# Levels 1 and 2 of the scores computed elementwise, from eight tokens side by side in a partition

## The chip, the cores and the metric

The kernel runs on one core of a Trainium2 chip. Times are device microseconds of that core. Before the change the median of three runs is 647.9 us (647.87 to 648.56). The engines are PE (matmuls), DVE (vector), ACT (scalar), POOL (GpSimd) and SP, which in this kernel computes nothing: it issues nearly all the DMAs, one after another, from one queue.

## The reference

```python
# r, k, v, w: 4 x 8 x 768 x 48 (batch, heads, tokens, head width); u: 8 x 48
for t in range(S):
    cur = np.einsum('bhd,bhe->bhde', u[None] * kt, vt)
    y[:, :, t] = np.einsum('bhd,bhde->bhe', rt, state + cur)
    state = wt[:, :, :, None] * state + np.einsum('bhd,bhe->bhde', kt, vt)
...
x = y.transpose(0, 2, 1, 3).reshape(B * S, H * D)   # 3072 x 384
h = x @ w_in                                        # 384 x 2048
out = (h * sigmoid(h)) @ w_out                      # 2048 x 384
```

A recurrence over the tokens of each head, in which the state decays by `w`, and then a two-layer network with a Silu on every token.

## The kernel before

The work is cut into 12 units: 128 tokens of two of the four batches, all 8 heads. For a unit the recurrence becomes a masked matrix of scores, tokens by tokens, for each head. Entry (query, key) is the sum over the head width of r times k times the product of all `w` between the two tokens. It is built by levels. Level l pairs the second half of every block of 2 << l tokens with its first half; before it is computed, queries in second halves and keys in first halves are multiplied by products of `w` that reach the middle of their block. Level 0 with the diagonal (the "bonus", which has `u`) is elementwise: a partition holds two neighbouring tokens, POOL multiplies (`bonus`, lines 398 to 410), DVE sums over the head width (`bonus_sum`, 412 to 419), four small DMAs move the sums to the partition of their key (422 to 425), ACT and DVE put them in order (`bonus_spread`, 440 to 445), and a predicated copy writes them into `score` (`bonus_write`, 447). Levels 1 to 6 are matmuls: `score_products` (519) runs 8 for a level, and two levels run together as a `burst` (601): 1 with 2, 3 with 4, 5 with 6. `keep_level` (609) copies a level from PSUM into `score` with a mask, on DVE. `grow_queries` (470, DVE) and `grow_keys` (476, POOL, with a copy on ACT in `odd_keys`, 458) multiply on to the next level, and `prepare` (587) makes the second level of a burst ready ahead of the first; `product` (383, POOL) makes the products of `w`. With `score` complete, `y` (655) multiplies scores and values, `update` (671) brings the state on, and `move_x` (707) takes the result to the network's layout with ten DMAs.

The network of a unit is `up` (752), eight steps of 12 matmul records each with a Silu on ACT into `gt`, and `quarter` (806), seven steps of 16 records that make the second product with fewer block products than the plain way, from sums that `sums` (796) forms on DVE.

The order is written by hand. For units 3 to 11 `mix` (725) lists groups of the recurrence's steps, and the loop at line 920 puts after each group as many network steps as `ROOM` (919) says: first the seven `quarter` steps of unit i - 2, then the eight `up` steps of unit i - 1. `sums` comes with the last four `up` steps, two of them with the last. Each engine works through its own instructions in this order. `y` comes in the last group, after all network steps. The loads of unit i + 2 (`load_blocks`, 97, 48 DMAs) are spread over the groups (line 742), and `load_rk` (128) brings r and k of the next unit for the bonus. All these, `move_x`, the bonus moves and the stores of the output are on SP's queue in the order of the program. Units 0 to 2 have an order of their own (861 to 917).

Of the kernel before, what the change touches and what calls it, by code (L numbers as in the profile page):

```python
# [8 lines left out]
F32 = mybir.dt.float32  # L9
BF16 = mybir.dt.bfloat16  # L10
I8 = mybir.dt.int8
I32 = mybir.dt.int32
# [26 lines left out]
def kernel(  # L39
# [11 lines left out]
    nc = tc.nc  # L51
# [14 lines left out]
    units = [(n, b0) for n in range(S // L) for b0 in range(0, B, NB)]  # L66
    NSLOT = 2
    NTOK = 2


    const = ctx.enter_context(tc.tile_pool(name="const", bufs=1))
# [15 lines left out]
    def load_twos(to, src, i, queues):  # L87
        n, b0 = units[i]
        for b in range(NB):
            queues[b].dma_start(out=to[b * L // 2:(b + 1) * L // 2],  # L90
                                in_=src[b0 + b, :, n * L:(n + 1) * L, :].rearrange("h (i s) d -> i h (s d)", s=2))
# [35 lines left out]

    def load_rk(i):

        for x, src in enumerate((r, k)):  # L130
            load_twos(tokens_rk[:, x].rearrange("p h s d -> p h (s d)"), src, i, [nc.sync] * NB)


    rounding = ExitStack()
# [19 lines left out]
    own = const.tile([128, NOWN, 2 * PW], U32, name="own")  # L154

    tokens_rk = const.tile([128, 2, H, 2, D], F32, name="tokens_rk")

    def rk(i, x):
        if i < NTOK:
# [77 lines left out]
    warm = const.tile([128, 1], F32, name="warm")  # L237
    nc.scalar.activation(out=warm, in_=zero, func=AF.Silu)
    u_bc = const.tile([128, H, D], F32, name="u_bc")
    nc.sync.dma_start(out=u_bc, in_=u.partition_broadcast(128))  # L240
    load_weight(0)
    load_tokens(1)
# [140 lines left out]
    def product(i, l, engine=nc.gpsimd):  # L383
        t = tw[i][l]
        up = pt.tile([128, Q, L >> (l + 1)], F32, name=f"tw{l + 1}", bufs=2 if l == NL - 1 else 1)
        engine.tensor_tensor(out=up, in0=t[:, :, 0::2], in1=t[:, :, 1::2], op=ALU.mult)  # L386
        tw[i].append(up)
# [24 lines left out]
    def bonus_sum(i, x):  # L412
# [10 lines left out]
        for b in range(NB):  # L423
            for s in range(2):
                nc.sync.dma_start(out=diag[i][b][s::2], in_=own_sums[b * L // 2:(b + 1) * L // 2, s])

    def bonus_spread(i):

        if i < NTOK:
            if i == 0:  # L430
                diag[i] = p_w[:, 0, 0:NB * H * 2].rearrange("p (b h s) -> p b h s", b=NB, h=H)
            else:
                diag[i] = ps.tile([128, NB, H, 2], F32, name="p_m", bufs=2)
            for b in range(NB):
                for s in range(2):
                    nc.tensor.matmul(diag[i][:, b].rearrange("p h s -> p (h s)"), lhsT=spread[:, s, b, :],
                                     rhs=own_sums[:, s].rearrange("p h s -> p (h s)"), start=(b == 0 and s == 0),
                                     stop=(b == NB - 1 and s == 1))
            return
        both_b = pt.tile([128, NB, H, 2], F32, name="both_b", bufs=1)  # L440
        nc.scalar.copy(out=both_b[:, 0], in_=diag[i][0])
        for g in range(4):
            nc.scalar.copy(out=both_b[(3 - g) * 32:(4 - g) * 32, 1], in_=diag[i][1][g * 32:(g + 1) * 32])
        nc.vector.stream_shuffle(out=both_b[:, 1], in_=both_b[:, 1], mask=list(range(31, -1, -1)))
        diag[i] = both_b
# [8 lines left out]
    def keys(i, start, *dims):  # L454
        k = tk[i][:]
        return bass.AP(tensor=k.tensor, offset=k.offset + start, ap=[k.ap[0], *dims])
# [16 lines left out]
        nc.vector.tensor_tensor(out=odd, in0=odd, in1=tw[i][l][:, :, 0::2][:, :, :, None].to_broadcast([128, Q, L >> (l + 1), c]),  # L473
                                op=ALU.mult)

    def grow_keys(i, l):
        c, ni = 1 << l, L >> (l + 1)
        x_at, next_at = X[l % 2], X[(l + 1) % 2]
        for b in range(NB):
            row0 = NP + b * NP  # L480
            if l + 1 < NL:
                start = [next_at * L, row0 * L][b] + b * c
                step = 2 * c + (1 - 2 * b) * (row0 - next_at) * L
                out = keys(i, start, [4 * c, NP * ni // 2], [step, 2], [1, c])
                have = keys(i, x_at * L + b * c, [4 * c, NP * ni // 2], [2 * c, 2], [1, c])
                blocks = [[4, NP * ni // 2], [2, 2]]
            else:
                out = keys(i, row0 * L + b * c, [L, NP], [1, c])
                have = keys(i, x_at * L + b * c, [L, NP], [1, c])
                blocks = [[2, NP]]  # L490
            nc.gpsimd.tensor_tensor(out=out, in0=have, in1=odd_products(i, l, b, *blocks), op=ALU.mult)  # L491
        if i < NTOK:
            product(i, l)

    def odd_ones(i):

# [200 lines left out]
    def dense_x(i, b):  # L697

        if b == 0:
            xt[i] = pt.tile([128, KC, TU], F32, name="xt")  # L700
        p_x = ps.tile([128, KC, L], F32, name="p_h" if i == 0 else "p_m", bufs=2)
        for x, (c, p) in enumerate(parts):
            nc.tensor.matmul(p_x[:, c, :], lhsT=dense[:, x, :], rhs=yt[i][:, p, b, :],  # L703
                             start=(x == 0), stop=(x == len(parts) - 1))
        (nc.vector.tensor_copy if (i, b) == (0, 1) else nc.scalar.copy)(out=xt[i][:, :, b * L:(b + 1) * L], in_=p_x)

    def move_x(i):

        xt[i] = pt.tile([128, KC, TU], F32, name="xt")
        for h in range(H):  # L710
            at = h * D
            while at < (h + 1) * D:
                end = min((h + 1) * D, (at // 128 + 1) * 128)
                row = PD * (h % 2) + at - h * D
                nc.sync.dma_start(out=xt[i][at % 128:at % 128 + end - at, at // 128, :],
                                  in_=yt[i][row:row + end - at, h // 2].rearrange("p b t -> p (b t)"))
                at = end

    def both(fn, i, *args):
        return [(fn, i, b, *args) for b in range(NB)]  # L720
# [4 lines left out]
    def mix(i):  # L725

        groups = [[*both(turn, i, "w"), (product, i, 0)],
                  [*both(turn, i, "k"), *both(turn, i, "r"), (odd_ones, i)], [(start_levels, i), (prepare_keys, i, 1)],
                  [(prepare, i, 1), *[(product, i, l) for l in range(1, NL)]],
                  [(burst, i, 1), (keep_level, i, 1)], [(keep_level, i, 2), (go_on, i, 2)],  # L730
                  [(prepare, i, 3), (reverse_v, i), (bonus, i, 0)],
                  [(burst, i, 3), (keep_level, i, 3), (bonus_sum, i, 0), (bonus, i, 1), (bonus, i, 2)],
                  [(keep_level, i, 4), (go_on, i, 4)],
                  [(prepare, i, 5), (bonus_sum, i, 1)] + ([(load_rk, i + 1)] if i + 1 < len(units) else []),
                  [(burst, i, 5), (keep_level, i, 5)], [(keep_level, i, 6), (go_on, i, 6), (bonus_spread, i), (bonus_write, i)],
                  both(turn_k, i), [*both(y_state, i), *both(y, i), *both(update, i), (move_x, i)]]

        loads = block_loads(i + NSLOT) if i + NSLOT < len(units) else []
        if i + 1 < len(units):
            loads.insert(len(loads) // 2, (load_values, i + 1))  # L740

        behind = groups[3 if i > NTOK + 1 else 10:]
        for at, group in enumerate(behind):
            group += loads[at * len(loads) // len(behind):(at + 1) * len(loads) // len(behind)]
        return groups
# [6 lines left out]
    def up(i, m):  # L752
        p_h = ps.tile([128, 2, TU], F32, name="p_h", bufs=2)
        for a in range(2):
            f = 2 * m + a
            for c in range(KC):
                nc.tensor.matmul(p_h[:, a, :], lhsT=w_in_sb[:, c, f * 128:(f + 1) * 128], rhs=xt[i][:, c, :],  # L757
                                 start=(c == 0), stop=(c == KC - 1))
        if i == 0 and m < NFIRST:
            gt[i, m] = own[:, NOWN - 1, m * 2 * TU:(m + 1) * 2 * TU].bitcast(F32).rearrange("p (a t) -> p a t", a=2)  # L760
        else:
            gt[i, m] = pt.tile([128, 2, TU], F32, name="gt", bufs=FC // 2 + 3)
        nc.scalar.activation(out=gt[i, m], in_=p_h, func=AF.Silu)  # L763

    def out_room(b):
# [138 lines left out]
    for m in range(6):  # L904
# [7 lines left out]
    do(blocks[2], (burst, 2, 3), (keep_level, 2, 3), (keep_level, 2, 4), (go_on, 2, 4), (prepare, 2, 5), (bonus, 2, 1),  # L912
       (bonus, 2, 2), (down, 0, 1, 2), (bonus_sum, 2, 1), (load_rk, 3), (sums, 1, 1), *blocks[3:7], (down, 0, 1, 3))
    do((burst, 2, 5), (keep_level, 2, 5), (keep_level, 2, 6), (go_on, 2, 6), (up, 1, 6), (bonus_spread, 2), (bonus_write, 2),
       (load_values, 3), *both(turn_k, 2), (weight_sums, 2), (up, 1, 7), (sums, 1, 2))
    do((sums, 1, 3), *both(y_state, 2), *both(y, 2), *both(update, 2), (move_x, 2),
       *blocks[7:])

    ROOM = 1, 1, 0, 2, 1, 1, 1, 1, 1, 2, 1, 2, 1, 0
    for i in range(3, len(units)):  # L920
        steps = downs(i - 2) + ups(i - 1)
        groups = mix(i)
        if i == NTOK + 1:

            groups[4].insert(1, (weight_sums, 3))
        for group, room in zip(groups, ROOM):
            do(*group)
            for step in steps[:room]:
                do(*step)
            steps = steps[room:]  # L930
# [32 lines left out]
```

## Time and profile before

| | before |
|---|---|
| median of the runs | 647.9 us |
| profiled execution: its span | 646.2 us |
| PE busy | 639.6 us, 99% |
| DVE, POOL, ACT busy | 433.9, 283.1, 203.8 us |
| starts of units 4, 5, 6, 7 (first `quarter` on PE) | 179.64, 230.58, 281.52, 332.46 us |
| start of the tail (last 22 network steps) | 585.73 us |
| mean granted PE clock | 1.000 |

The span is that of one profiled execution, from its first instruction to its last; the runs' times are 1.7 us longer. A matmul in 32 bits shows as two records. In the views of the prediction a row is a group or a merged piece of instructions: line of the kernel, engine, operation, output <- input, count. In rows by form the part between the bars is busy time in us and mean ns of one, and what follows is the idle time of the engine before them and what ended it.

### The profile page before, as it was taken

To read this page: it belongs to the slowest core of one execution; us is meant where nothing else is said; L and a number is where in the kernel's file an instruction comes from. 1 tells how busy PE (TensorE), PEld (TensorE's weight loads), DVE (VectorE), ACT (ScalarE), POOL (GpSimd) and SP (SyncE) were. 2 spreads that over 40 slices of the span, in tenths; PEclk is the share of its full clock that TensorE was granted. 3 is DMA by queue.
4 is the path that set the end of the run, shared out by engine and by line. 5 is a ranking of instruction groups with operands and counts; after the bars stand their busy time and mean duration, and the time that the engine had idled before them with its cause. 6 is when DMAs were issued, how large, how long until landed. Compare 5 with 4: busy or idle time off the path is not lost.

```text
span 646.2 us, 12889 instructions
## 1 busy us (share of the span) xinstructions
PE 639.6 (99%) x4878; PEld 579.2 (90%) x4878; DVE 433.9 (67%) x737; ACT 203.8 (32%) x408; POOL 283.1 (44%) x356
## 2 busy tenths in 40 slices
PE   8999999999999999999999999999999999999998
PEld 7888876898899899899899899899899989989997
DVE  7879789896777677586586586676586766751031
ACT  5798872212321321320321231231232232131120
POOL 6898398466065054254334425416416505510000
PEclk9999999999999999999999999999999999999999
DMA  9975954433534524513513513423432022000000
GB/s 229 276 180 131 229 129 50 91 75 52 96 63 69 96 49 72 88 31 64 98 29 67 96 28 58 96 37 52 90 54 38 26 50 50 27 2 25 25 0 25
DMA packets 201134, 49.21 MB, mean 76 GB/s; under 512 B 188912, under 2 KB 195952, under 8 KB 201072
## 3 DMA queue, kind: packets, MB, share of 16 engines
q1 hardware_dynamic: 199488, 47.79, 36.5%
q10 hardware_dynamic: 1584, 0.59, 0.4%
q8 instruction: 39, 0.64, 0.4%
q14 instruction: 23, 0.19, 0.1%
HBM read 39.52 MB, written 4.72 MB: 68 GB/s over the span
## 4 chain that ended last, share of the span: by engine, by line
PE 95%; DVE 2%; POOL 1%; ACT 1%; issue 1%; POOLq 0%; DVEq 0%; ACTq 0%
PE p_h L757 39%; PE p_o L820 31%; PE p_sc L527 6%; PE p_m L527 4%; PE p_m L776 3%; PE p_m L665 3%; PE p_m L652 3%; PE p_m L639 1%; PE p_sc L679 1%; POOL tk L491 1%; PE p_m L350 1%; PE p_m L855 1%; PE p_m L703 0%; DVE score L450 0%; POOL w_in_sb L227 0%
## 5 line engine op out<-in xcount | busy, mean ns | idle before, releaser
L757 PE MATMUL p_h<-xt,w_in_sb 128*128 128x256 f32 x1152 | 258.4, 382 | 0.7 <-POOL tk L507 0.7
L757 PEld LDWEIGHTS p_h<-xt,w_in_sb 128*128 128x128 f32 x1152 | 215.8, 190 | 32.5 <-POOL tk L507 0.9
L763 ACT ACTIVATE gt<-p_h 128x512 f32<-128x512 f32 x93 | 55.5, 596 | 228.2 <-PE p_h L757 228.1
L491 POOL TENSOR_TENSOR tk<-tk,tw 128x256 f32<-128x256 f32 x144 | 102.1, 732 | 23.3 <-ACT tk L461 16.6
L537 DVE COPY_PREDICATED score<-mask,p_sc 128x512 f32<-128x512 int8 x78 | 64.1, 885 | 59.7 <-PE p_sc L527 59.4
L820 PE MATMUL p_o<-own,temps 128*128 128x192 f32 x528 | 90.3, 328 | 0.4 <-DVE temps L829 0.4
L820 PE MATMUL p_o<-w_out_sb,gt 128*128 128x192 f32 x528 | 90.4, 328 | 0.0
L820 PEld LDWEIGHTS p_o<-own,temps 128*128 128x128 f32 x528 | 85.8, 190 | 1.8 <-DVE temps L829 0.7
L820 PEld LDWEIGHTS p_o<-w_out_sb,gt 128*128 128x128 f32 x528 | 85.9, 190 | 0.9 <-issue 0.4
L684 POOL TENSOR_TENSOR state<-state,tw 128x512 f32<-128x512 f32 x16 | 19.3, 1225 | 118.5 <-PE p_m L652 118.5
L386 POOL TENSOR_TENSOR tw<-tw 128x256 f32<-128x256 f32 (+6 forms) x83 | 39.8, 480 | 54.5 <-DVE tw L338 50.6
L802 DVE TENSOR_TENSOR temps<-gt 128x256 f32<-128x256 f32 x88 | 44.3, 504 | 21.9 <-ACT gt L763 21.9
L461 ACT COPY tk<-tk 128x256 f32<-128x256 f32 x60 | 24.6, 410 | 83.4 <-PE p_sc L527 40.8
L527 PEld LDWEIGHTS p_sc<-tr,tk 48*128 48x128 f32 x640 | 39.2, 186 | 12.1 <-issue 8.9
L473 DVE TENSOR_TENSOR tr<-tr,tw 128x512 f32<-128x512 f32 x53 | 46.0, 868 | 3.3 <-POOL tk L491 1.0
L527 PE MATMUL p_sc<-tr,tk 48*128 48x128 f32 x640 | 47.1, 285 | 0.6 <-POOL tk L491 0.6
L408 POOL TENSOR_TENSOR ruk<-tokens_rk 128x768 f32<-128x768 f32 x10 | 18.6, 1858 | 65.8 <-DVE own_sums L415 65.8
L595 DVE TENSOR_TENSOR tr<-tr,tw 128x512 f32<-128x512 f32 x29 | 39.9, 1375 | 1.3
L537 DVE COPY_PREDICATED score<-mask,p_m 128x512 f32<-128x512 int8 x54 | 35.4, 706 | 0.0
L820 PE MATMUL p_o<-w_out_sb,temps 128*128 128x192 f32 x176 | 30.4, 326 | 0.0
L829 DVE TENSOR_TENSOR partial<-p_o,partial 128x192 f32<-128x192 f32 x33 | 11.6, 353 | 27.6 <-PE p_o L820 27.6
L597 ACT COPY tr<-tr 128x512 f32<-128x512 f32 x29 | 18.4, 634 | 35.8 <-DVE tr L473 35.0
(144 smaller groups left out, 753.3 us busy)
## 6 DMA issues: line engine op xcount, KB each, us to landing
w_out_sb<-in_moe_w_in_dram SPq DMA_DIRECT2D x6, 768.0 KB, 6.9
tokens_rk<-in_r_dram SPq DMA_DIRECT2D x20, 192.0 KB, 3.4
tokens_rk<-in_k_dram SPq DMA_DIRECT2D x20, 192.0 KB, 3.8
w_out_sb<-in_moe_w_out_dram SPq DMA_DIRECT2D x4, 768.0 KB, 6.3
own<-in_moe_w_out_dram SPq DMA_DIRECT2D x4, 768.0 KB, 5.8
xt<-yt SPq DMA_DIRECT2D x60, 48.0 KB, 2.0
raw<-in_w_dram SPq DMA_DIRECT2D x80, 32.0 KB, 2.2
raw<-in_k_dram SPq DMA_DIRECT2D x80, 32.0 KB, 2.4
```

The source lines that it names most:

```text
L386: engine.tensor_tensor(out=up, in0=t[:, :, 0::2], in1=t[:, :, 1::2], op=ALU.mult)
L461: nc.scalar.copy(out=keys(i, X[(l + 1) % 2] * L + c, [4 * c, blocks], [c, 2], [1, c]), in_=keys(i, NP * L + c, [4 * c, blocks], [NP * L + ...
L473: nc.vector.tensor_tensor(out=odd, in0=odd, in1=tw[i][l][:, :, 0::2][:, :, :, None].to_broadcast([128, Q, L >> (l + 1), c]), op=ALU.mult)
L491: nc.gpsimd.tensor_tensor(out=out, in0=have, in1=odd_products(i, l, b, *blocks), op=ALU.mult)
L527: nc.tensor.matmul(bass.AP(tensor=s_p.tensor, offset=s_p.offset, ap=[s_p.ap[0], [apart * L // 2, 2], [1, L // 2]]), lhsT=tk[i][rows, X[l % ...
L537: nc.vector.copy_predicated(out=dst, mask=masks[l][:, :, None].to_broadcast([128, NB, NP, ni, c]), data=sc[e].rearrange("p (b q) (i c) -> ...
L595: nc.vector.tensor_tensor(out=new[:, :, :, 1, :], in0=old[:, :, :, 1, :], in1=tw[i][l][:, :, 0::2][:, :, :, None].to_broadcast([128, Q, L ...
L652: nc.tensor.matmul(p_yt[i, b][:, p, :], lhsT=state[:, b0 + b, p, :], rhs=tr[i][:, b * NP + p, :], start=(p == 0), stop=False)
L757: nc.tensor.matmul(p_h[:, a, :], lhsT=w_in_sb[:, c, f * 128:(f + 1) * 128], rhs=xt[i][:, c, :], start=(c == 0), stop=(c == KC - 1))
L763: nc.scalar.activation(out=gt[i, m], in_=p_h, func=AF.Silu)
L802: nc.vector.tensor_tensor(out=out, in0=one, in1=two, op=op)
L820: nc.tensor.matmul(p, lhsT=left(f), rhs=right[:, f, :], start=(f == 0), stop=(f == FH - 1))
```

## The change

From unit 3 on a partition holds eight neighbouring tokens of a pair of heads, of r, k and w, and levels 0, 1 and 2 are all computed from them by POOL (`block_bonus`, eight steps) and summed by DVE (`block_sum`, five steps). Eight DMAs (`block_move`) take the sums to the partition of their key, `block_spread` puts them in order, and `block_write` writes them into `score` with a mask that `make_block_mask` prepares in unit 3. The burst of levels 1 and 2 is gone, with its masked copies. `grow_own` multiplies queries and keys over levels 0 and 1 in place. `load_rk` loads the three tensors with 24 DMAs, `load_u` lays `u` out anew once, and `mix` has 13 groups instead of 14, with another `ROOM`. `xt` has one buffer instead of two, `gt` 8 instead of 11; a new tile `spare` of three such places holds part of unit 1's `gt` and, from unit 3 on, the data of the new steps.

```diff
     def load_rk(i):
-        for x, src in enumerate((r, k)):
-            load_twos(tokens_rk[:, x].rearrange("p h s d -> p h (s d)"), src, i, [nc.sync] * NB)
+        if i < NPAIR:
...
+        for to, src in ((eights[0], r), (eights[1], k), (eights[2], w)):
+            for b in range(NB):
+                for g in range(NP):
+                    at = (b * NP + g) * (L // BLK)
+                    nc.sync.dma_start(out=to[at:at + L // BLK].rearrange("p e s d -> p e (s d)"),
+                                      in_=src[b0 + b, 2 * g:2 * g + 2, n * L:(n + 1) * L, :].rearrange(
+                                          "e (i s) d -> i e (s d)", s=BLK))
...
+    def load_u():
+        for b in range(NB):
+            for g in range(NP):
+                at = (b * NP + g) * (L // BLK)
+                nc.sync.dma_start(out=u_bc[at:at + L // BLK, 0:2], in_=u[2 * g:2 * g + 2].partition_broadcast(L // BLK))
...
+    def make_block_mask():
...
+    def block_bonus(i, step):
+        mul = lambda out, one, two: nc.gpsimd.tensor_tensor(out=out, in0=one, in1=two, op=ALU.mult)
+        W = BLK * D
+        if step == 0:
+            ruk[i] = pt.tile([128, 2 * W], F32, name="ruk", bufs=1)
+            mul(ruk[i], at_rk(R_AT, [1, 2 * W]), at_rk(K_AT, [1, 2 * W]))
+        elif step == 1:
+            mul(have, have, u_bc[:, 0:2][:, :, None, :].to_broadcast([128, 2, BLK, D]))
...
+        else:
+            e = step - 6
+            to = (room_b, ruk[i])[e]
+            mul(to.rearrange("p (k q d) -> p k q d", k=4, q=4), at_rk(K_AT + e * W, [D, 4], [0, 4], [1, D]),
+                at_rk(R_AT + e * W + 4 * D, [0, 4], [D, 4], [1, D]))
...
+    def block_sum(i, step):
+        add = lambda out, have: nc.vector.tensor_reduce(out=out, in_=have, axis=mybir.AxisListType.X, op=ALU.add)
...
+    def block_move(i):
+        for b in range(NB):
+            for g in range(NP):
+                at = (b * NP + g) * (L // BLK)
+                nc.sync.dma_start(out=block_diag[b][:, g * 2 * BLK:(g + 1) * 2 * BLK],
+                                  in_=block_sums[at:at + L // BLK].rearrange("p s e q -> p s (e q)"))
+
+    def block_spread(i):
+        flat = block_both.rearrange("p b h s -> p b (h s)")
+        nc.scalar.copy(out=flat[:, 0], in_=block_diag[0])
+        for g in range(4):
+            nc.scalar.copy(out=flat[(3 - g) * 32:(4 - g) * 32, 1], in_=block_diag[1][g * 32:(g + 1) * 32])
+        nc.vector.stream_shuffle(out=flat[:, 1], in_=flat[:, 1], mask=list(range(31, -1, -1)))
+
+    def block_write(i):
+        shape = [128, NB, NP, L // BLK, BLK]
+        for e in range(2):
+            nc.vector.copy_predicated(out=score[:, i % NSC, e].rearrange("p (b q) (i s) -> p b q i s", b=NB, s=BLK),
+                                      mask=block_mask[:, :, None].to_broadcast(shape),
+                                      data=block_both[:, :, e::2][:, :, :, None, :].to_broadcast(shape))
...
+    def grow_own(i, l):
+        c, ni = 1 << l, L >> (l + 1)
+        for b in range(NB):
+            have = keys(i, (NP + b * NP) * L + b * c, [2 * c, NP * ni], [1, c])
+            nc.gpsimd.tensor_tensor(out=have, in0=have, in1=odd_products(i, l, b, [2, NP * ni]), op=ALU.mult)
+        grow_queries(i, l)
...
     def mix(i):
         groups = [[*both(turn, i, "w"), (product, i, 0)],
-                  [*both(turn, i, "k"), *both(turn, i, "r"), (odd_ones, i)], [(start_levels, i), (prepare_keys, i, 1)],
-                  [(prepare, i, 1), *[(product, i, l) for l in range(1, NL)]],
-                  [(burst, i, 1), (keep_level, i, 1)], [(keep_level, i, 2), (go_on, i, 2)],
-                  [(prepare, i, 3), (reverse_v, i), (bonus, i, 0)],
-                  [(burst, i, 3), (keep_level, i, 3), (bonus_sum, i, 0), (bonus, i, 1), (bonus, i, 2)],
-                  [(keep_level, i, 4), (go_on, i, 4)],
-                  [(prepare, i, 5), (bonus_sum, i, 1)] + ([(load_rk, i + 1)] if i + 1 < len(units) else []),
-                  [(burst, i, 5), (keep_level, i, 5)], [(keep_level, i, 6), (go_on, i, 6), (bonus_spread, i), (bonus_write, i)],
-                  both(turn_k, i), [*both(y_state, i), *both(y, i), *both(update, i), (move_x, i)]]
+                  [*both(turn, i, "k"), *both(turn, i, "r"), (grow_own, i, 0)],
+                  [*[(product, i, l) for l in range(1, NL)], (grow_own, i, 1)],
+                  [(odd_keys, i, 2), (grow_keys, i, 2, False), (grow_queries, i, 2)], [(prepare, i, 3)],
+                  [(burst, i, 3), (keep_level, i, 3), (block_bonus, i, 0), (block_bonus, i, 1)],
+                  [(keep_level, i, 4), (go_on, i, 4), *[(make_block_mask,)] * (i == NPAIR), (block_bonus, i, 2), (block_bonus, i, 3),
+                   (block_sum, i, 0)],
+                  [(prepare, i, 5), (reverse_v, i), (block_bonus, i, 4), (block_sum, i, 1)],
+                  [(block_bonus, i, 5), (block_bonus, i, 6), (block_sum, i, 2)],
+                  [(burst, i, 5), (keep_level, i, 5), (block_bonus, i, 7), *[(load_rk, i + 1)] * (i + 1 < len(units))],
+                  [(block_sum, i, 3), (keep_level, i, 6), (go_on, i, 6), (block_sum, i, 4), (block_move, i)],
+                  both(turn_k, i), [(block_spread, i), (block_write, i), *both(y_state, i), *both(y, i), *both(update, i), (move_x, i)]]
...
-       (load_values, 3), *both(turn_k, 2), (weight_sums, 2), (up, 1, 7), (sums, 1, 2))
+       (load_values, 3), (load_u,), *both(turn_k, 2), (weight_sums, 2), (up, 1, 7), (sums, 1, 2))
...
-    ROOM = 1, 1, 0, 2, 1, 1, 1, 1, 1, 2, 1, 2, 1, 0
+    ROOM = 1, 1, 1, 1, 2, 1, 1, 1, 2, 1, 2, 1, 0
```

## The prediction

> **What bounds the kernel now.** I read the page first: busy time per engine, then the chain that ended last.
>
> ```profile
> PE 639.6 (99%) x4878; PEld 579.2 (90%) x4878; DVE 433.9 (67%) x737; ACT 203.8 (32%) x408; POOL 283.1 (44%) x356
> PE 95%; DVE 2%; POOL 1%; ACT 1%; issue 1%; POOLq 0%; DVEq 0%; ACTq 0%
> ```
>
> PE is the bound, and the clock is 1.00, so what leaves PE leaves the time, as long as nothing else arrives late. The chain in order of time shows one steady unit (start us, us, instructions):
>
> ```profile
> 281.52 10.60 PE p_o L820 x64
> 292.12 1.11 PE p_sc L527 x16
> 293.22 0.89 PE p_m L527 x16
> ...
> 328.07 1.78 PE p_m L652 x16
> 329.86 1.88 PE p_m L665 x32
> ...
> 332.46 10.60 PE p_o L820 x64
> ```
>
> A unit is 50.9 us without a gap; a burst of two levels is 1.11 + 0.89 = 2.0 us. Line 665 (`y`) reads `score` and starts 48.3 us into the unit. Next, the timeline of SP, which issues all the loads (start us, us):
>
> ```profile
> 434.28 6.92 SPq L715 DMA_DIRECT2D xt<-yt  x10
> 441.54 3.86 SPq L106 DMA_DIRECT2D raw<-in_r_dram  x8
> ...
> 462.98 2.45 SPq L425 DMA_DIRECT2D diag<-own_sums  x4
> 465.52 1.36 SPq L90 DMA_DIRECT2D tokens_rk<-in_r_dram  x2
> 466.92 1.31 SPq L90 DMA_DIRECT2D tokens_rk<-in_k_dram  x2
> 468.28 4.79 SPq L106 DMA_DIRECT2D raw<-in_k_dram  x8
> 473.11 4.01 SPq L106 DMA_DIRECT2D raw<-in_r_dram  x8
> 485.22 6.88 SPq L715 DMA_DIRECT2D xt<-yt  x10
> ```
>
> The queue is a straight line: each DMA holds it until the next can go. From start to start a `raw` load costs (445.50 - 441.54)/8 = 0.495 us (445.50 is the next row's start), an SBUF to SBUF move (465.52 - 462.98)/4 = 0.635, a `tokens_rk` load (468.28 - 465.52)/4 = 0.69, an output store 0.41 (452.75 to 453.16 in the same view). All rows of this unit sum to 40.3 us: SP has only some 10 us to spare, all of it in waits for `yt`, sums and outputs. Two or three issues in a unit take about 0.9 us more than their fellows. Durations of the compute, by form:
>
> ```profile
> L491 POOL TENSOR_TENSOR tk<-tk,tw 128x256 f32<-128x256 f32 x144 | 102.1, 732 | 23.3 <-ACT tk L461 16.6 <-DVE tw L386 3.2 <-PE p_sc L527 1.5
> L450 DVE COPY_PREDICATED score<-own_mask,both_b 128x1024 f32<-128x1024 int8 x20 | 25.0, 1304 | 0.3
> L410 POOL TENSOR_TENSOR ruk<-ruk,u_bc 128x768 f32<-128x768 f32 x10 | 21.4, 2141 | 0.8
> L408 POOL TENSOR_TENSOR ruk<-tokens_rk 128x768 f32<-128x768 f32 x10 | 18.6, 1858 | 65.8 <-DVE own_sums L415 65.8
> L406 POOL TENSOR_TENSOR ruk<-tokens_rk 128x384 f32<-128x384 f32 x10 | 10.6, 1062 | 0.0
> ```
>
> **The Trainium skill.** "DMA: Bandwidth & Descriptors", Anatomy of one DMA: the DMA engines do not wait on semaphores, the wait "happens on the issuing sequencer before dispatch"; the trace agrees, SP stands 8.1 us before line 715 waiting for `yt` with nothing behind it issued. The same section puts most of a small DMA's 2 us into the receipt of its write; here `diag` lands 1.7 us after issue. "TensorE: Matmul & The Clock Gate", Part 1: after an idle window of about 3.4 us the PE clock halves until about 3.4 us of work have passed; no run here shows it, since PE never idles that long.
>
> **The change part by part** (units 3 to 11; T is a unit's first `quarter`).
>
> PE loses one burst of 16 matmuls, two records each: 9 x 2.0 = 18 us, down to a 48.9 us unit with `y` at T+46.3. DVE loses four predicated copies (2.47 + 1.29 us in one unit) and gets 3456 instead of 1152 elements of reduction (0.5 us per 384): about -0.8 us of 35, not a bound. POOL swaps 5.0 us of bonus for 14 (below) and saves about 1 on keys: 29 us of a unit. Neither is full. `gt` with 8 and `xt` with 1 buffer I cost at nothing: their old readers are matmuls that PE, in order, has passed, and 7 quarters (18 us) cover the new `xt`; without that cover each unit would wait some 8 us (6.3 issue + 2 landing).
>
> SP: `load_rk` goes from 4 DMAs to 24 (2.8 to 24 x 0.495 = 11.9 us) and `block_move` has 8 instead of 4 (5.1 instead of 2.5). The unit's 40.3 become 52.0 us, already more than PE's 48.9. The price of the new load is unseen: 16 partitions, two runs of 1536 B. I take 0.495, which `raw` and `v` share; bounds 0.41 (the store) and 0.69 (the old `tokens_rk`).
>
> Worse is the order. `load_rk(i+1)` overwrites tokens that the last `block_bonus` reads, so SP stops there until POOL has done step 7; queued behind are 8 `raw` loads, then `block_move`, whose data `block_write` needs before `y`. When is step 7 done? POOL in order, from T: product 0 starts at 2.7 as before and takes 1.04 (3.8); `grow_own` 0, two at about 0.9 (5.6); six products 2.35 (7.9); `grow_own` 1, 1.5 (9.4); copy on ACT, then `grow_keys` 2, 0.65 + 1.5 (11.6); the same for 3 (13.7); bonus steps 0 and 1, 1.85 + 2.14 (17.7). `grow_keys` 4 needs burst 3: six quarters of 2.65 and 2.0 make 17.9, plus the ACT copy 18.5, plus 1.5: 20.0. Steps 2 and 3, 1.0 each (22.0). `grow_keys` 5 needs an ACT copy that stands behind the first Silu: PE 17.9 + 2.65 + 2.65, then 0.6 + 0.4 + 0.2 gives 24.4, plus 1.5: 25.9. Step 4, two of 384 elements, 2.0; step 5, four of 192 at about 0.57, 2.3; steps 6 and 7, 1.85 each: **T+34**. SP itself gets there at about T+31, so POOL is late, narrowly.
>
> From there: `load_rk` 11.9 (45.9), 8 loads 4.0 (49.9), `block_move`: the eighth issues 7 x 0.635 = 4.4 later and lands after 1.7 (56.0), four ACT copies 0.8 (56.9), shuffle 0.2 (57.2), two predicated copies of 1.3, of which `y` needs both (59.8). From the first `y` to the next `move_x` the timelines show 332.40 - 329.79 = 2.6: 62.4. With about 1.2 for slow issues among these 40 DMAs and 1.5 for a halved clock over `y` (0 to 2.5; its matmuls take 1.9 at full clock), a unit is **65 us**; PE idles some 14 us ahead of `y`. The bonus sums are not the holdup: burst 5 ends at T+32.9, the last reduction at about T+37.5.
>
> Sum, in the profiled execution (unit 3 starts at 128.0). The stage ahead issues `load_rk(3)` and 8 DMAs of `load_u`, 9.1 + 3.6 us more, so `move_x(2)` slips from 134.9 to 147.6 and lands at 156; the first `up` wanted it at 148.6. Step 7 follows that `up`: 169; loads to 181, no `raw` between, `y` from 191, unit 4 at 196. In unit 3 33 loads stand between `block_move` and `move_x`, so SP starts unit 4 about 9 us late, reaches `load_rk` at 237 instead of 230, and unit 5 starts at 267.5. Units 5 to 9: 5 x 65 = 325 (592.5). Unit 10 has no `raw` loads, 61 (653.5). Unit 11 loads nothing, but `block_write` waits behind the last `sums`: 53 (706.5). The tail is 646.2 - 585.7 = 60.5: 767. The median of the runs lies 1.7 above this span: **768**.
>
> With the load at 0.41, -0.085 x 24 x 8 = -16, and no clock loss, -12: 740. At 0.69, +37, and a clock loss of 2.5, +8: 813. That is the likeliest case's own range.
>
> **Rivals.** (1) Faster, 630: PE stays the bound and only the 18 us go. For this `block_move` must start by 46.3 - 2.6 - 0.3 - 0.9 - 6.1 = T+36.4. Step 7 at T+34 and 16 us of loads ahead of it speak against; it would take loads that cost nothing and POOL 2 us sooner. (2) Slower but mildly, 668: the queue has room after all (the wait of `load_rk` falls on an earlier reader, and loads issue faster), and only the place of `block_write` counts. It stands on DVE behind the `sums` of the last `up`, whose Silu ends at T+44.9; in the DVE timeline the last `sums` took 328.74 to 331.88, 3.1 us, then 2.7 of shuffle and copies: `y` at T+50.5 instead of 46.3, 4.2 lost against 2.0 won, 9 x 2.2 = +20. It is certain to be paid where SP is not later. (3) POOL is quicker than reckoned and SP's own rate decides: load at T+31 instead of T+34, 8 x 3 less, 744. (4) That the burst is not saved: excluded, the changed program's PE list has 16 fewer score matmuls in each of these units.
>
> **How the numbers follow.** The queue mechanism, with (3) in it, has 0.86, of which 0.76 in 740 to 813; (2) 0.09; (1) 0.04, 0.01 for anything within 0.2% (1.3 us, about what a measurement of this kernel can tell from no change). The range goes from 722 to 822 to take in more of the tails of the mechanism's sum; (1) and (2) stay outside. Faster 0.04, same 0.01, slower 0.95.
>
> **What would show it.** Right: SP waits at `load_rk` for POOL's bonus product in units 5 to 9; 24 issues at about 0.5 us; `block_move` starting near T+50; ACT's spread copies waiting for these DMAs; PE idle about 14 us ahead of `y`, released by the predicated copy; units of 65 us. Wrong: `block_move` at T+38 right after the last reduction (rival 2), or PE without gaps (rival 1). The prediction also fails if the small loads issue at well under 0.4 us.

## The result and the profile after

| | before | after |
|---|---|---|
| median of the runs | 648.1 us | 752.2 us (751.3 to 752.6) |
| ratio, 95% interval | | 1.161 (1.159 to 1.162) |
| span of the profiled execution | 646.2 us | 750.9 us |
| mean granted PE clock | 1.000 | 0.932 |
| units 3 to 11, us each | 50.9 (steady) | 63.9, 71.7, 63.5, 62.9, 61.4, 63.1, 63.2, 58.5, 53.5 |

The kernel became 104 us slower. First the page of the kernel after: span, busy time, the clock in 40 slices, and the group of `y` (busy us, mean ns, then idle time of PE ahead of it and its releaser).

```profile
span 750.9 us, 12562 instructions
...
PE 646.3 (86%) x4590; PEld 582.0 (78%) x4590; DVE 407.7 (54%) x750; ACT 189.4 (25%) x381; POOL 359.3 (48%) x421
...
PEclk9999999989999599879979979987997997999999
...
L812 PE MATMUL p_m<-score,vt 128*48 128x128 f32 (+1 forms) x176 | 25.1, 395 | 93.6 <-DVE score L562 93.6
```

No engine is full any more. PE has 288 records fewer, yet 6.7 us more busy time: 18 us went with the bursts, so about 25 came from matmuls at a lower clock (run eight below, with the same records at a mean clock of 0.992, is busy 623.0 us). It stood 93.6 us for `y`, released by `block_write` (562): 88.5 ahead of its first record and 5.1 behind its second, where it waits for the second of the two copies. Together: -18 + 25 + 93.6, and 3.3 us of `up` waiting for `xt` in unit 3, are 104 of the 104.7 us between the spans.

The chain that ended last carries no reading here: the page follows it through 8% of the span only. So I read one unit, the one that starts at 390.6, in the timelines (start us, us, engine, line, pieces). SP:

```profile
418.57 3.24 SPq L129 DMA_DIRECT2D vq<-in_v_dram  x4
422.76 3.58 SPq L142 DMA_DIRECT2D tokens_rk<-in_r_dram  x8
426.37 3.69 SPq L142 DMA_DIRECT2D tokens_rk<-in_k_dram  x8
430.11 3.70 SPq L142 DMA_DIRECT2D tokens_w<-in_w_dram  x8
433.85 3.87 SPq L109 DMA_DIRECT2D raw<-in_k_dram  x8
437.83 5.10 SPq L548 DMA_DIRECT2D spare<-spare  x8
...
452.03 6.26 SPq L862 DMA_DIRECT2D xt<-yt  x10
```

POOL's last two bonus products in this unit:

```profile
419.14 1.81 POOL L493 TENSOR_TENSOR spare<-tokens_rk 128x768 f32<-128x768 f32 x1
420.91 1.82 POOL L493 TENSOR_TENSOR ruk<-tokens_rk 128x768 f32<-128x768 f32 x1
```

And PE around `y` (in brackets the idle time before a piece and its releaser):

```profile
434.86 1.95 PE L799 MATMUL p_m<-tr,state 128*128 128x128 f32 x16
...
446.86 0.66 PE L812 MATMUL p_m<-score,vt 128*48 128x128 f32 x2 [10.06 <-DVE score L562]
448.05 1.73 PE L812 MATMUL p_m<-score,vt 128*48 128x128 f32 x13 [0.52 <-DVE score L562]
...
452.03 5.47 PE L972 MATMUL p_o<-w_out_sb,gt 128*128 128x192 f32 x32
```

The last product ends at 422.73; 0.03 us later the first token load goes out. The moves (548) whose data `y` needs start 15 us after that, behind 24 token loads and 8 raw ones that nobody needs yet. PE has nothing to do for 10.06 us, and then `y`, 32 records, takes from 446.86 to 451.4, 4.5 us in place of 1.9: 0.5 is the wait for the second copy, and the mean granted clock over these 4.5 us is 0.55.

In SP's waits the wait for POOL is small (total, times, longest); 10.6 of it falls in unit 10, which has no `raw` loads:

```profile
SPq L142 <- POOL ruk L493: 19.3, 7, 10.6
```

So there are four suspects in one stretch: the wait for POOL, the number of issues, their place in the queue, and the place of `block_write` on DVE.

### The profile page after: what moved, and what is told of

Its sections match the earlier page's. It is cut to its first block, busy times and chain, and to the rows that moved or that the text cites. A ratio compares the mean times of both kernels' runs of the same rounds, so it can differ in the third digit from the quotient of the medians.

```text
span 750.9 us, 12562 instructions
## 1 busy us (share of the span) xinstructions
PE 646.3 (86%) x4590; PEld 582.0 (78%) x4590; DVE 407.7 (54%) x750; ACT 189.4 (25%) x381; POOL 359.3 (48%) x421
## 3 DMA queue, kind: packets, MB, share of 16 engines
q1 hardware_dynamic: 198592, 51.84, 33.1%
## 5 line engine op out<-in xcount | busy, mean ns | idle before, releaser
L812 PE MATMUL p_m<-score,vt 128*48 128x128 f32 (+1 forms) x176 | 25.1, 395 | 93.6 <-DVE score L562 93.6
L812 PEld LDWEIGHTS p_m<-score,vt 128*48 128x48 f32 (+1 forms) x176 | 17.0, 179 | 99.5 <-DVE score L562 98.8
L630 POOL TENSOR_TENSOR tk<-tk,tw 128x256 f32<-128x256 f32 x126 | 85.7, 701 | 17.5 <-PE p_sc L674 7.8
L684 DVE COPY_PREDICATED score<-mask,p_sc 128x512 f32<-128x512 int8 x60 | 42.1, 755 | 53.3 <-PE p_sc L674 53.0
L954 DVE TENSOR_TENSOR temps<-gt 128x256 f32<-128x256 f32 x84 | 42.0, 500 | 48.3 <-ACT gt L915 48.3
L493 POOL TENSOR_TENSOR ruk<-tokens_rk 128x768 f32<-128x768 f32 (+1 forms) x36 | 52.8, 1477 | 16.1 <-DVE spare L527 16.1
L612 DVE TENSOR_TENSOR tr<-tr,tw 128x512 f32<-128x512 f32 x62 | 46.8, 755 | 3.6 <-POOL tk L630 1.1
L674 PEld LDWEIGHTS p_sc<-tr,tk 48*128 48x128 f32 x496 | 30.4, 187 | 10.1 <-issue 7.0
L674 PE MATMUL p_sc<-tr,tk 48*128 48x128 f32 x496 | 36.5, 285 | 0.7 <-POOL tk L630 0.6
L527 DVE TENSOR_REDUCE spare<-ruk 128x4 f32<-128x192 f32 (+1 forms) x54 | 27.2, 545 | 10.4 <-POOL ruk L493 10.4
L981 DVE TENSOR_TENSOR temps<-p_o,partial 128x192 f32<-128x192 f32 x22 | 7.9, 358 | 43.9 <-PE p_o L972 31.8
```

The costliest lines, as they stand in the source:

```text
L493: mul = lambda out, one, two: nc.gpsimd.tensor_tensor(out=out, in0=one, in1=two, op=ALU.mult)
L527: add = lambda out, have: nc.vector.tensor_reduce(out=out, in_=have, axis=mybir.AxisListType.X, op=ALU.add)
L674: nc.tensor.matmul(bass.AP(tensor=s_p.tensor, offset=s_p.offset, ap=[s_p.ap[0], [apart * L // 2, 2], [1, L // 2]]), lhsT=tk[i][rows, X[l % ...
L684: nc.vector.copy_predicated(out=dst, mask=masks[l][:, :, None].to_broadcast([128, NB, NP, ni, c]), data=sc[e].rearrange("p (b q) (i c) -> ...
L812: nc.tensor.matmul(p_yt[i, b][PD * e:PD * e + width, p, :], lhsT=whole[i][b][:, h * D:h * D + width], rhs=score[:, i % NSC, e, b * NP + p, ...
L954: nc.vector.tensor_tensor(out=out, in0=one, in1=two, op=op)
```

## The experiments

All kernels are variants of the changed one. Runs one to five and seven are one execution each; of six, eight and nine the median of four is given. "T" is the start of a unit, and units 5 to 9 are the steady ones (63 us in the kernel after).

**One: the place alone.** The token loads go behind the moves.

```diff
-  [(burst, i, 5), (keep_level, i, 5), (block_bonus, i, 7), *[(load_rk, i + 1)] * (i + 1 < len(units))],
-  [(block_sum, i, 3), (keep_level, i, 6), (go_on, i, 6), (block_sum, i, 4), (block_move, i)],
+  [(burst, i, 5), (keep_level, i, 5), (block_bonus, i, 7)],
+  [(block_sum, i, 3), (keep_level, i, 6), (go_on, i, 6), (block_sum, i, 4), (block_move, i),
+   *[(load_rk, i + 1)] * (i + 1 < len(units))],
```

> The changed kernel with one step moved: load_rk(i+1) is listed after block_move instead of before it, so SP issues the eight moves first and the 24 loads behind them. Nothing else is changed. Theory (SP's queue holds block_move back): block_move starts when the last reduction is done, about T+37.5 as in unit 11 of the changed kernel (37.9) instead of T+47 to T+49; y is then held only by the late block_write, units of about 53.5 to 54 us in the steady part, units 3 and 4 near 60 and 70 because the queue is still behind there; about 697 us. Rival (the order on the queue is not what counts: the time went to POOL's products, or to block_write's place): units stay at 61 to 63 us, 745 to 755 us.

Measured 705.8 us: 46 us of the loss are the place. Steady units take 55.4 us, a little more than the 53.5 to 54 expected. The moves now start at T+37, 10 us sooner, but `block_write` only some 7 us sooner (T+48.4), for it has a new releaser. DVE in the unit at 371.0 of this kernel:

```profile
416.11 0.42 DVE L955 TENSOR_TENSOR temps<-gt 128x256 f32<-128x256 f32 x1 [1.91 <-ACT gt L916]
...
418.84 0.41 DVE L955 TENSOR_TENSOR temps<-gt,temps 128x256 f32<-128x256 f32 x1
419.18 0.01 DVE L556 LOAD_MASK_SELECT spare<-spare  x1
419.18 0.21 DVE L556 STREAM_SHUFFLE spare<-spare 128x64 f32<-128x64 f32 x1
419.43 2.47 DVE L562 COPY_PREDICATED score<-spare 128x1024 f32<-128x1024 int8 x2
```

The shuffle follows the last `sums` with no idle time before it: the data were there, DVE's order held them.

**Two: no token loads at all** in units 4 to 11 (`load_rk` returns), so no wait for POOL and no issues.

> The changed kernel without load_rk for units 4 to 11 (their bonus works on the tokens of unit 3, so those outputs are not the reference's): the 24 issues and SP's wait for POOL's last product are both gone, all else stays. Theory: block_move at about T+38, unit 53.5 as unit 11 measures in the changed kernel, about 678 us; what is left over 630 is the late block_write, 53.5 - 48.9 = 4.6 us a unit. Rival (POOL's 14 us of products or the eight moves hold the unit): units of 58 us or more, over 715 us.

Measured 692.2 us, steady units 55.5. It stays under the rival's 715: what the loads cost in the changed kernel is 60 us, and no more than that. It is 14 us above the expectation, which took the 53.5 us of the changed kernel's unit 11 for every unit. The slow clock is hardly a part of this difference, for `y` takes 4.5 us in that unit too. In the unit that starts at 360.5 of this run, 54.9 us, `y` starts at T+49.8, 3.6 us after PE's last work, against T+49.1 and 2.0 us in unit 11, and 0.65 us of state update follow it, which unit 11 does not have. Unit 4, where the moves go out only at T+42.3, takes 57.4.

**Three: the same, with the write before the last `up` and its `sums`.**

```diff
-  both(turn_k, i), [(block_spread, i), (block_write, i), *both(y_state, i), ...
+  [*both(turn_k, i), (block_spread, i), (block_write, i)], [*both(y_state, i), ...
```

> The kernel without load_rk for units 4 to 11, and with block_spread and block_write listed with turn_k, ahead of the last up and of the last two sums, instead of behind them. Theory: with the sums out of the way the write follows the landing of the moves (about T+44.8), ACT's copies and the shuffle: written at about T+48.6 instead of T+50.2, unit about 51.3, about 660 us. Rival (the sums were not in the way, the landing of the moves is): no change against the run without loads, about 678 us.

Measured 667.3 us, 25 less; units 6 to 9 take 50.7 to 50.9 us, unit 5 53.5. DVE in this kernel now waits for the data (released by ACT's copy of the moved sums), not the data for DVE:

```profile
399.02 0.01 DVE L558 LOAD_MASK_SELECT spare<-spare  x1 [3.84 <-ACT spare L557]
399.28 3.33 DVE L564 COPY_PREDICATED score<-spare 128x1024 f32<-128x1024 int8 x2
```

**Four: the wait for POOL kept, a third of the issues.** Only the 8 loads of r are issued in units 4 to 11; those of k and w are left out.

```diff
-        for to, src in ((eights[0], r), (eights[1], k), (eights[2], w)):
+        for to, src in ((eights[0], r), (eights[1], k), (eights[2], w))[:3 if i == NPAIR else 1]:
```

> The changed kernel with load_rk cut to the eight loads of r for units 4 to 11 (k and w stay those of unit 3, so those outputs are not the reference's); the wait for POOL's last product stays in its place. It parts the wait from the issues. Theory (both add up on one queue): 16 issues of 0.47 us less, block_move at about T+40 instead of T+47.2 to 48.9, unit about 54.5, about 688 us. Rival (the wait for POOL is the cost, the number of issues is not): still 60 us a unit or more, over 730 us.

Measured 692.7 us, the same as with no loads. The wait alone costs nothing here: SP stands until T+32 as in the kernel after, but the moves then start at T+39.8, early enough for the last `sums` to be what `block_write` waits for. So it is the issues behind the wait, not the wait.

**Five: both orders mended, everything loaded.** The last sums and the moves come before the last kept level, the token loads behind the moves, the write before the last `up`.

```diff
-  [(burst, i, 5), (keep_level, i, 5), (block_bonus, i, 7), *[(load_rk, i + 1)] * (i + 1 < len(units))],
-  [(block_sum, i, 3), (keep_level, i, 6), (go_on, i, 6), (block_sum, i, 4), (block_move, i)],
-  both(turn_k, i), [(block_spread, i), (block_write, i), *both(y_state, i), ...
+  [(burst, i, 5), (block_bonus, i, 7), (block_sum, i, 3), (block_sum, i, 4), (block_move, i), (keep_level, i, 5)],
+  [*[(load_rk, i + 1)] * (i + 1 < len(units)), (keep_level, i, 6), (go_on, i, 6)],
+  [(block_spread, i), *both(turn_k, i), (block_write, i)], [*both(y_state, i), ...
```

> Nothing is left out; only places are changed. The moves are issued ahead of the token loads, as in the run that moved them first, and besides POOL's sums of levels 3 and 4 come ahead of the last kept level, and VectorE writes the shuffled blocks ahead of the last pair of update matmuls and their sums. Theory that SP's own rate becomes the bound once its order is mended: SP still issues the 24 loads of tokens, 8 of blocks, 8 moves and all the rest in every unit, about 52 us at the pitch that the trace shows and 2 us for the slow issues among them, which is more than the 49 us of TensorE: units of 54 us and 685 to 690 us in all (plus or minus 8). Rival, that the order alone was the cause: units of 50 us as without loads and an early write or less, 660 us or below; with no remainder 637.

Measured 677.4 us, the low edge of the first theory and far from 637. Steady units take 52 to 57 us. SP in one of them, from one `move_x` to the next:

```profile
368.16 6.26 SPq L862 DMA_DIRECT2D xt<-yt  x10
...
395.55 5.28 SPq L548 DMA_DIRECT2D spare<-spare  x8
400.88 4.04 SPq L109 DMA_DIRECT2D raw<-in_k_dram  x8
405.02 4.70 SPq L142 DMA_DIRECT2D tokens_rk<-in_r_dram  x8
409.76 3.69 SPq L142 DMA_DIRECT2D tokens_rk<-in_k_dram  x8
413.50 3.69 SPq L142 DMA_DIRECT2D tokens_w<-in_w_dram  x8
417.24 3.88 SPq L109 DMA_DIRECT2D raw<-in_r_dram  x8
421.21 7.16 SPq L862 DMA_DIRECT2D xt<-yt  x10
```

97 issues in 53.05 us and hardly a gap: the moves go out at T+39.6, though their sums are ready near T+33, because SP gets to them no sooner. In units 10 and 11, where fewer loads are left, they go out at T+33.1 and the unit takes 48.0 us.

**Six: part of the issues moved to ACT's queue.** The 8 loads of w (`queue=nc.scalar`, listed after the first turn) and the 5 of v, with the raw loads spread otherwise.

> Nothing is left out. The order of the run before, and 8 loads of w tokens a unit and the 5 of v are issued from ACT's queue in place of SP's, and the raw loads are spread ahead of the moves and behind the loads of tokens, some into the next unit. Theory (SP's order first, its rate second, TensorE third): SP has about 13 issues of 0.45 us fewer, 46 us a unit, so TensorE is the bound again, units of 49.5 us from unit 3 on except a longer start: 128.5 + 9 x 49.6 + 60.6 + 1.3 = 637 us, faster than before. Rival, that something else still holds y back (the write behind VectorE's sums, ACT's queue delayed by its new issues): units of 52 us or more, 660 us and above, not faster than before (648).

Measured 702.5 us (ratio to before 1.083, 1.082 to 1.085): worse than five. It is not faster than before, as the rival had it. Some of PE's and SP's longest waits in this kernel (total, times, longest):

```profile
PE p_m L806 <- ACT kq L794: 34.7, 7, 9.5
PE p_h L917 <- DMA xt<-yt: 15.1, 10, 3.7
SPq L109 <- DMA tokens_w<-in_w_dram: 47.2, 8, 9.4
SPq L869 <- DMA vt<-in_v_dram: 23.9, 6, 5.5
```

PE waits for `kq`, which ACT copies only after the moved sums, and for `xt`; the moves and `move_x` are both on SP's queue. SP's timeline at the start of the unit at 431.0:

```profile
430.66 9.37 SPq L109 DMA_DIRECT2D raw<-in_k_dram  x8
440.13 10.20 SPq L869 DMA_DIRECT2D xt<-yt  x10
```

ACT and its queue at the same time:

```profile
433.87 0.32 ACT L990 COPY partial<-p_o 128x192 f32<-128x192 f32 x1 [2.92 <-PE p_o L983]
433.93 3.65 ACTq L149 DMA_DIRECT2D tokens_w<-in_w_dram  x8
```

Eight raw loads, 3.9 us elsewhere, took 9.4. SP starts them at 430.66 and waits for the landing of `tokens_w` loads that ACT has not issued yet: ACT issues them from 433.93 on, for it stands at its own place behind a matmul. The raw loads neither read nor write `tokens_w`; what ties them to these landings no view of the profile shows. The rival's second point, that ACT is delayed by its new issues, is in the trace too, but smaller: ACT's copies of `tk` wait 22.3 us, in 7 waits, for the loads of v. What the other spread of the raw loads added is not separated: it put 40 raw loads between `move_x` and the moves, which start at T+41 to T+44.

**Seven: fewer issues, everything else as in the changed kernel.** Heads and batches follow each other at one stride in memory, so one DMA can fill all 128 partitions for one head of each pair: 6 token loads of 192 KB for 24 of 48 KB.

```diff
-            for b in range(NB):
-                for g in range(NP):
-                    at = (b * NP + g) * (L // BLK)
-                    nc.sync.dma_start(out=to[at:at + L // BLK].rearrange("p e s d -> p e (s d)"), ...
+            for e in range(2):
+                first = src[b0, e, n * L:n * L + 1, 0:1]
+                nc.sync.dma_start(out=to[:, e].rearrange("p s d -> p (s d)"),
+                                  in_=bass.AP(tensor=first.tensor, offset=first.offset,
+                                              ap=[[2 * S * D, NB * NP], [BLK * D, L // BLK], [1, BLK * D]]))
```

> Nothing is left out and no place is changed: the changed kernel, with its 24 loads of tokens of 16 partitions each made 6 of 128 partitions (the same bytes, the same place in SP's order, the same wait for POOL). Theory that the number of SP's issues sets y's place: load_rk takes 6 x 0.5 = 3 us in place of 11, the moves go out at T+40 in place of 47.2, early enough for VectorE's last sums to hold the write, so about the time of the run with the r loads alone, 692 us (plus or minus 8). Rival, that the bytes or the wait for POOL set it and not the count of issues: 735 us or more.

Measured 698.5 us: the same bytes, and the second load of r still goes out only when POOL's last product is done (T+32), and 54 us less. SP of this kernel (unit at 363.3):

```profile
394.34 1.78 SPq L141 DMA_DIRECT2D tokens_rk<-in_r_dram  x2
396.18 1.24 SPq L141 DMA_DIRECT2D tokens_rk<-in_k_dram  x2
397.46 1.24 SPq L141 DMA_DIRECT2D tokens_w<-in_w_dram  x2
398.75 6.54 SPq L109 DMA_DIRECT2D raw<-in_k_dram  x8
405.38 5.09 SPq L547 DMA_DIRECT2D spare<-spare  x8
```

Six loads take 4.4 us, not the 3 expected, and the eight behind them 6.5 instead of 3.9: SP's waits put 10.5 us of this kernel to raw loads that wait for `tokens_w` to land. The moves start at T+42, not T+40.

**Eight: six loads with the orders of five.**

> Nothing is left out. The order of the run that moved POOL's sums, the moves and the write, and the 24 loads of tokens made 6. Theory that SP's rate was what was left there: SP issues 79 a unit in place of 97, about 40 us, well below TensorE's 49, so the moves go out at T+33 as in that run's units 9 and 10 (48.0 us each), every unit takes 48.5 to 50 us, and the longer units 3 and 4 (56.6 and 65.4 there) shrink to 52: 128.5 + 2 x 52 + 7 x 49 + 60.5 + 1.7 = 638 us (plus or minus 8), faster than before. Rival, that something other than SP holds those units: 660 us or more, slower than before.

Measured 644.1 us, ratio to before 0.9947 (0.9931 to 0.9964): 0.5% faster than before, and 33 us less than five by the issues alone. Its page, busy time:

```profile
PE 623.0 (97%) x4590; PEld 564.0 (88%) x4590; DVE 405.4 (63%) x750; ACT 188.3 (29%) x381; POOL 357.8 (56%) x421
```

PE at the end of the unit at 339.1:

```profile
383.34 1.95 PE L798 MATMUL p_m<-tr,state 128*128 128x128 f32 x16
385.22 1.08 PE L811 MATMUL p_m<-score,vt 128*48 128x128 f32 x16
386.13 1.04 PE L811 MATMUL p_m<-score,vq 128*48 128x128 f32 x16
```

`y` follows without a gap and takes 1.9 us; units 5 to 9 take 48.7 us each. PE's busy time is 16.6 us under that of before: the change's own saving. The distance to the expected 638 comes from unit 4: 62.5 us, from 179.1, where 52 were expected. It contains the one long wait that is left among PE's; the line of ACT behind it shows that ACT, before it copies `kq`, stood 8.6 us for the moves, which SP sends only at T+48.3:

```profile
PE p_m L798 <- ACT kq L786: 9.9, 1, 9.9
231.26 0.24 ACT L552 COPY spare<-spare 128x64 f32<-128x64 f32 x1 [8.60 <-DMA spare<-spare]
```

SP issues in it without a pause from 175 to 232, of which these rows:

```profile
193.78 7.05 SPq L861 DMA_DIRECT2D xt<-yt  x10
...
219.99 4.72 SPq L109 DMA_DIRECT2D raw<-in_k_dram  x8
...
227.41 5.10 SPq L547 DMA_DIRECT2D spare<-spare  x8
```

**Nine: the raw loads of units 3 to 10 spread anew**, some ahead of unit 3's moves, some put off by a unit.

```diff
+        if i + 1 < len(units):
+            groups[4].append((load_values, i + 1))
...
+        ahead, behind = {3: (4, 2), 4: (5, 2), 5: (6, 2)}.get(i, (8, 2))
+        groups[2] += late.pop(i, [])
+        late[i + 1] = loads[ahead + behind:]
+        for at, load in enumerate(loads[:ahead]):
+            groups[8 if i == 3 else 3 + at * 6 // ahead].append(load)
+        groups[10] += loads[ahead:ahead + behind]
```

> Nothing is left out. The kernel with six loads, the order and the write moved, and SP's raw loads spread anew: in unit 3 four groups of them (16 issues) ahead of the moves, where SP stood idle 7 us, two behind the token loads, six put off to unit 4; units 4 and 5 put off 5 and 4 more groups, later ones 2. Theory that unit 4's 62.5 us is SP's backlog alone (52 us without a pause from 175 to 227, the moves at T+48.3): the moves of unit 4 go out at about T+33 to 36, unit 4 takes 49 to 51 us, TensorE's wait of 9.9 us for y goes, the rest stays: 644.1 - 12 to 13 = 632 us (plus or minus 4). Rival, that unit 4 is long because of its own late start of POOL or late xt: 640 us or more.

Measured 639.4 us (637.3 to 641.2), ratio to before 0.987 (0.984 to 0.989). Unit 4 takes 48.8 us, so its length was SP's backlog; but part of the backlog moved. Unit 3 grew from 51.0 to 57.7 us, and unit 6 from 48.8 to 51.1. SP in it:

```profile
162.22 9.06 SPq L109 DMA_DIRECT2D raw<-in_w_dram  x16
171.39 5.11 SPq L547 DMA_DIRECT2D spare<-spare  x8
```

The gap that they were to fill was 7.2 us (159.0 to 166.2 in run eight). The loads of v, which the same edit lists earlier, took 2.5 of it, and the 16 loads 9.1 where 7.8 were reckoned: too much, and the moves slipped from T+38.1 to T+43.2. What unit 4 gained, units 3 and 6 gave back in part: the gain is 4.7 us of the 12 expected, and the theory's 632 (plus or minus 4) is missed.

## Why the prediction was right, step by step

The direction, the mechanism and its place were right; the time was 16 us too high, inside the range.

- **The queue decides, by place and by count.** Right, and shown from two sides. Changing the place only (one) takes 46 us off, changing the count only (seven) 54, and taking the loads away (two) 60.
- **The wait for POOL, "late, narrowly".** The wait is there in 7 units (3 and 5 to 10), and it ends at T+32.1 to T+32.5 in units 5 to 10, not T+34. The terms that were mis-sized: the product with `u` takes 1.82 us, not 2.14, and two key products of the later levels 1.2, not 1.5. Run four shows that the wait by itself costs nothing. The prediction's narrow rival of 744, in which SP's own rate decides, was therefore not a separate case but the next layer of the same one.
- **24 loads by 0.495.** Mis-sized: in the unit read above the 24 take from 422.76 to 433.85, 0.462 each; one of them is busy 0.422 us. The moves start at T+47.2 to T+48.9 in units 5 to 9, not T+49.9.
- **The slow clock, "1.5 (0 to 2.5)" a unit.** Mis-sized the other way: PE is busy 50.9 to 51.7 us in units 5 to 9 where 48.9 were reckoned, 2.4 more on average. (Of the 25 us in all, 5.5 are in unit 3.) The idle time ahead of `y`, put at some 14 us in such a unit, is 10.1 to 11.4. The first error took back part of the second. The Trainium skill, "TensorE: Matmul & The Clock Gate", Part 1, which the trace of before could not show, agrees with the unit read above: the granted clock falls to 0.50 some 4 us after PE has run dry and is 1.00 again some 4 us after `y` has begun. Its idle window of about 3.4 us is no lower limit here, though: the last section has idle times of 2.0 us that were enough.
- **Sum of the steady units.** 5 x 65 = 325 predicted, 314.1 measured: 10.9 of the 16 us. Unit 3 was 63.9, not 68: `up` starts on the first pieces of `xt` and waits 3.3 us in three parts, where the prediction let it wait 7.4 for the last piece. Unit 4 (71.7 for 71.5), with SP at `load_rk` at T+42, and the tail (60.6 for 60.5) came as reckoned; unit 10 was 2.5 us shorter. That unit 11 took 53.5 us for 53 is luck: `y` starts at T+49.1, not T+50.5, and then takes 4.5 us at the slow clock, which the prediction did not give this unit.
- **`block_write` behind the last `sums`** (rival 2). The place was right (run one shows it as soon as the queue allows), the price too low: 692 us without any loads, not 668. The prediction's own terms (44.9, 3.1 and 2.7) sum to `y` at T+50.7, not T+50.5, a small slip. What it left out is the clock: in run two PE idles 3.6 us and `y` takes 4.3 to 4.8 us in place of 1.9, so that units 5 to 9 are 55.5 us and not 53.1, 12 us in all. Most of the rest is unit 3, 64.1 us, where the moves go out only at T+46.
- **SP's 52.0 us a unit, "already more than PE's 48.9".** Right: 53.05 us measured in run five, and a unit bound by it.
- **Rival 1, 630 us.** The 18 us of PE were real: 48.7 us a unit in run eight. What kept it away was what the prediction named against it. The smaller `gt` and `xt`, costed at nothing, are in run eight too, and PE has no gap in its units 5 to 9 and waits 1.3 us in all for `xt`. DVE's time fell from 35.1 to 32.1 us a unit, not by the 0.8 reckoned; it was no bound either way.

Layer by layer from 752.2: the place of the loads 46.4 (705.8), the place of the write and of the last sums 28.4 (677.4), the number of issues 33.3 (644.1), the spread of the raw loads 4.7 (639.4). The layers were taken off in this order; in another order the shares differ, as the 54 us of run seven show. What stays open is what ties SP's loads to ACT's in run six, how much of its loss is this tie and how much its spread of loads, and whether unit 3 can be brought to 49 us as well.

## What to carry to other kernels

Count the DMA issues of a stage, multiply by the pitch in the trace and compare with the stage's bound; where the sum comes near, try fewer and larger DMAs: 6 loads for 24, with the same bytes, took off 54 us here before the order was mended and 33 after. On an in-order queue a load that is early for its reader may be late for the one behind it: put what the next matmul waits for ahead of prefetches, and on the consuming engine ahead of work that is not urgent. A small idle time on PE can cost more than its length: 3.6 us of it cost `y` nearly 2 us more in run two.

## What the runs showed of the hardware

- The issue of a load of four times the bytes took only 1.4 to 1.6 times as long: SP was busy 0.42 us with one of 16 partitions of 2 x 1536 B (48 KB; kernel after) and 0.60 to 0.67 with one of 128 partitions of 1536 B (192 KB; run seven). The Trainium skill, "DMA: Bandwidth & Descriptors", Issuing engines are not separate DMA queues, calls the time to initiate a DMA "usually small relative to the DMA itself". That is so for each one here, 0.42 us against 2.0 from issue to landing; but the landings overlap and the issues do not, so that 97 of them in a unit were the bound in run five (53 us), with the DMA engines busy 37% of the span.
- An idle time of 3.6 us ahead of `y` (run two) cost nearly as much clock as one of 10 us (the kernel after): PE is busy 3.7 and 4.0 us with the same records in place of 1.95.
- An idle time of 2.0 us ahead of `y`, with another of 0.8 behind its second record, occurs nine times. The granted clock fell to 0.50 in five of them (unit 11 of the kernel after, 10 and 11 of run one, 10 of runs four and seven) and stayed at 1.00 in the four others (10 and 11 of run two, 11 of runs four and seven).
- In run six loads on SP's queue waited 47 us for loads issued from ACT's queue, whose tile they do not touch. The profile shows this only as one queue's DMA waiting for another's landing, and not why.
